# Channel attention and gated convolution on one core: depthwise weights converted early, later softmaxes partly on GpSimd, a new schedule of the score groups

## Chip, cores, metric

One Trainium2 chip, one core. The metric is the device time of a whole execution in microseconds (us); the kernel before took a median of 656.28 us over 3 runs (656.17 to 656.32). The engines are named as the profile names them: PE is TensorE (PEld its weight loads), DVE is VectorE, ACT is ScalarE, POOL is GpSimd, SP is the engine that issues the loads.

## What is computed

B = 4 batches, N = 6336 rows, C = 256 channels, float32; the three weights of the second half come as float64.

```python
qn = q / (norm(q, axis=1) + 1e-6)              # over the N rows, for each channel
kn = k / (norm(k, axis=1) + 1e-6)
s = kn.transpose(0, 2, 1) @ qn / tau           # 256 x 256 for each batch
a = exp(s - max(s)); a /= a.sum(-1) + 1e-9
x = v @ a
gate = sigmoid(causal depthwise conv of x, 5 taps: conv_w)
out = (gate * (x @ w_val)) @ w_out
```

## The kernel before

**Two passes that overlap.** For each batch a first pass reads q and k, adds up the scores k^T q in PSUM (s_ps) and the sums of squares for the norms. A softmax then makes the weights a, and the product of a with w_val, both kept as a high and a low half (float32r). The second pass reads v in 13 chunks of 508 rows, which are the steps: 4 batches x 13 = 52 steps. While the steps of a batch run, the scores of the next batch are added up between them.

**Score groups.** Rows of q and k come in 17 groups of a batch, of three 128-row pieces each (group 0 has two; group 3 two and the 64 left over). `score_group` splits pieces into a high half (a ScalarE cast, L223) and a low half (a GpSimd subtraction, L224), three float32r products each; "plain" pieces are multiplied as float32, without a split (`nw` pieces of a group). In batch 0 two pieces of a group are plain (all of the first four groups); in batch 1 two of each group below `LEAD`. The squares (L236, L240) are on ScalarE, their sums on VectorE and GpSimd (L246). `split_group` emits split and squares of the next group and issues loads (4 groups ahead), `run_group` emits the products of a group that has been split.

**Softmax.** `softmax(b)` is a generator; each `tick` emits its next piece at high priority. It joins the sums (L276), sums over partitions on TensorE (L281, L283) into a PSUM tile with a bank of its own, takes square roots there (L288), adds and inverts (L292 to L294), scales the scores (L299), takes the minimum (L301) and the exponentials (L304, with their sum z), scales them to a (L311), splits a (L314, L315), transposes it (L321) and multiplies it with w_val (L330 to L335).

**A step.** `step` n: sigmoid of chunk n, convolution of chunk n+1 (`conv`: product x_ps, first tap on ScalarE L395, four taps on VectorE L397), value product (`value`, L415), split of the gated value (`split_g`: g_hi on ScalarE L428, g_lo on GpSimd L429), transposes of v two chunks ahead (`transpose_v`, L371 to L373), and the output product of chunk n-1 (`finish`, L445, L455). PSUM has four banks for all tiles with tag "bank" (o_ps, t_ps, val_ps, the softmax's tiles) and two for x_ps.

**Weights.** The float64 weights are loaded as pairs of int32 words and decoded on VectorE (`decode`, L145 to L159, then L165, L167): w_val into wa, w_out into wb, the five taps (10 rows: 5 taps x 2 halves of the channels) into wk. The taps are then transposed on TensorE (L185) and copied to cw (L186). Taps and w_val are loaded at group 5 and decoded from group 9 of batch 0 on, one step of each for every group.

**What sets the order.** The code is written in the order of the main loop, and a scheduler then orders each engine's instructions; `tc.high_priority`, `tc.issue_after` and `behind(...)` (not before the marked instruction) steer it. How many groups run in a step comes from `due`, a straight line from the 22 groups done when the steps begin to all 68 at step 35: one or two a step, without a pause at the end of a batch. In each engine the instructions then start in that order.

## Time and profile before

| | us |
|---|---|
| median of 3 runs | 656.28 |
| the profiled execution | 654.72 |
| its span, first to last instruction | 652.9 |

The views used below: the page (busy time of each engine and its share of the span; the granted clock of TensorE in 40 slices, 9 being full speed to within a tenth), the waits (who waited for whom: us in total, times, longest), busy time by stretch of the span, groups of instructions by line (busy us, mean ns | idle us before them), the timeline (start, length, engine, line, instruction, and in brackets the idle time before it and what ended it), and the chain of waits that ended last (start, length, engine, line). In the timeline and in chains a row with x8 stands for eight instructions in a row. A float32 product of 256 columns is two records of the trace, one of float32r is one.

### The profile page before, as it was taken

How to read it: one execution, taken by the hardware profiler on the slowest of the kernel's cores; microseconds unless marked ns; L12 is line 12 of the kernel's file. 1: busy time of each engine (PE TensorE's matmuls, PEld its weight loads, DVE VectorE, ACT ScalarE, POOL GpSimd, SP SyncE). 2: the span in 40 equal slices, each digit the busy share in tenths (PEclk: the TensorE clock that was granted, in tenths of full speed). 3: DMA queues.
4: the chain of work that ended last, by engine and by line, in shares of the span. 5: the costliest groups of instructions: out<-in, count | busy, mean ns of one | idle time of the engine just before them, and what ended most of it. 6: DMA issues, size and time to landing. Idle time of an engine off the chain costs nothing.

```text
span 652.9 us, 10789 instructions
## 1 busy us (share of the span) xinstructions
PE 636.3 (97%) x4051; PEld 573.7 (88%) x4051; DVE 530.0 (81%) x849; ACT 472.5 (72%) x622; POOL 366.6 (56%) x177
## 2 busy tenths in 40 slices
PE   9899899999999999999998999999999999999996
PEld 7788799998988999999997998999999798888886
DVE  3998998887888688778887788778778889888884
ACT  5588978867898778678699777777777755655564
POOL 1674597956747759559575387766763122312221
PEclk9999999999999999999998999999999999999999
DMA  8989754454646464545563374553222343443213
GB/s 294 396 277 357 262 204 140 156 188 136 193 114 192 147 208 162 193 125 184 152 188 119 112 240 147 184 180 103 65 81 71 118 126 97 121 129 106 65 43 108
DMA packets 73817, 105.78 MB, mean 162 GB/s; under 512 B 4442, under 2 KB 55844, under 8 KB 73764
## 3 DMA queue, kind: packets, MB, share of 16 engines
q1 hardware_dynamic: 47988, 79.76, 37.0%
q10 hardware_dynamic: 25776, 25.32, 13.9%
q8 instruction: 32, 0.52, 0.3%
q14 instruction: 21, 0.17, 0.1%
HBM read 79.11 MB, written 25.95 MB: 161 GB/s over the span
## 4 chain that ended last, share of the span: by engine, by line
PE 79%; DVE 10%; ACT 5%; DMA 3%; issue 1%; POOL 1%; SPq 0%; ACTq 0%; DVEq 0%
PE o_ps L445 20%; PE x_ps L381 19%; PE val_ps L381 19%; PE s_ps L262 14%; PE t_ps L371 6%; DVE acc_ps L246 4%; DMA raw<-in_k_dram 2%; DVE gate L397 1%; ACT sq L240 1%; PE o_ps L330 1%; DMA out_dram<-o_sb 1%; ACT hi L223 1%; POOL hi L224 1%; DVE gate L415 1%; ACT gate L403 0%
## 5 line engine op out<-in xcount | busy, mean ns | idle before, releaser
L397 DVE SCALAR_TENSOR_TENSOR gate<-x_ps,cw,gate 128x508 f32<-128x508 f32 (+1 forms) x416 | 275.4, 718 | 14.2 <-ACT gate L395 13.1
L224 POOL TENSOR_TENSOR hi<-raw,hi 128x1536 fp32r<-128x1536 f32 (+2 forms) x65 | 182.9, 2816 | 115.4 <-ACT hi L223 115.4
L429 POOL TENSOR_TENSOR g_lo<-gate,g_hi 128x1016 fp32r<-128x1016 f32 (+1 forms) x50 | 116.7, 2335 | 143.1 <-ACT g_hi L428 133.2
L246 DVE TENSOR_TENSOR acc_ps<-acc_ps,sq 128x512 f32<-128x512 f32 (+1 forms) x142 | 98.7, 695 | 66.8 <-ACT sq L240 64.3
L381 PE MATMUL x_ps<-v_hi,w 128*128 128x512 f32 (+1 forms) x416 | 139.3, 394 | 0.3 <-DVE gate L397 0.3
L262 PE MATMUL s_ps<-hi 128*128 128x256 f32 (+1 forms) x918 | 133.4, 289 | 5.8 <-ACT hi L223 3.0
L381 PE MATMUL val_ps<-v_hi,w 128*128 128x508 f32 (+1 forms) x416 | 133.6, 383 | 0.7 <-ACT o_sb L455 0.7
L262 PEld LDWEIGHTS s_ps<-hi 128*128 128x128 f32 (+1 forms) x918 | 120.6, 190 | 11.8 <-POOL hi L224 3.8
L455 ACT COPY o_sb<-o_ps 128x512 f32<-128x512 f32 x99 | 58.2, 589 | 77.9 <-PE o_ps L445 77.7
L445 PE MATMUL o_ps<-wo_hi,g_hi 128*128 128x256 f32 x400 | 113.1, 283 | 0.2 <-DVE gate L415 0.2
L445 PE MATMUL o_ps<-wo_lo,g_hi 128*128 128x256 f32 x400 | 112.1, 280 | 0.0
L445 PE MATMUL o_ps<-wo_hi,g_lo 128*128 128x256 f32 x400 | 111.6, 279 | 0.0
L240 ACT ACTIVATE sq<-raw 128x1536 f32<-128x1536 f32 (+2 forms) x72 | 96.4, 1343 | 11.1 <-DVE acc_ps L246 8.6
L381 PEld LDWEIGHTS x_ps<-v_hi,w 128*128 128x128 f32 x416 | 78.2, 190 | 14.6 <-PE s_ps L262 0.4
L381 PEld LDWEIGHTS val_ps<-v_hi,w 128*128 128x128 f32 x416 | 77.2, 188 | 14.4 <-ACT o_sb L455 0.9
L395 ACT ACTIVATE gate<-x_ps,cw 128x508 f32<-128x508 f32 (+1 forms) x104 | 68.2, 670 | 19.8 <-PE x_ps L381 19.3
L372 ACT CAST v_hi<-t_ps 128x512 fp32r<-128x512 f32 (+1 forms) x104 | 55.6, 568 | 35.9 <-PE t_ps L371 35.9
L381 PE MATMUL x_ps<-v_lo,w 128*128 128x512 f32 (+1 forms) x208 | 80.3, 386 | 0.0
L381 PE MATMUL val_ps<-v_lo,w 128*128 128x508 f32 (+1 forms) x208 | 79.2, 381 | 0.0
L223 ACT CAST hi<-raw 128x1536 fp32r<-128x1536 f32 (+2 forms) x65 | 77.6, 1200 | 1.8 <-DMA raw<-in_k_dram 1.1
L415 DVE TENSOR_TENSOR gate<-val_ps,gate 128x508 f32<-128x508 f32 (+1 forms) x104 | 64.3, 658 | 18.0 <-ACT gate L403 12.8
L445 PEld LDWEIGHTS o_ps<-wo_hi,g_hi 128*128 128x128 f32 x400 | 75.2, 188 | 1.4 <-DVE gate L415 0.4
(99 smaller groups left out, 787.1 us busy)
## 6 DMA issues: line engine op xcount, KB each, us to landing
raw<-in_q_dram SPq DMA_DIRECT2D x60, 384.0 KB
raw<-in_k_dram SPq DMA_DIRECT2D x60, 384.0 KB
v_raw<-in_v_dram SPq DMA_DIRECT2D x44, 512.0 KB
out_dram<-o_sb ACTq DMA_DIRECT2D x47, 384.0 KB
out_dram<-o_sb ACTq DMA_DIRECT2D x47, 124.0 KB
raw<-in_q_dram SPq DMA_DIRECT2D x8, 256.0 KB
raw<-in_k_dram SPq DMA_DIRECT2D x8, 256.0 KB
v_raw<-in_v_dram SPq DMA_DIRECT2D x4, 384.0 KB
```

Of the source, the lines that this page charges most:

```text
L223: cast = nc.scalar.copy(hi[r, js, :, 0, :], rows_of[r, js])
L224: nc.gpsimd.tensor_tensor(hi[r, js, :, 1, :], rows_of[r, js], hi[r, js, :, 0, :].bitcast(F32), ALU.subtract)
L240: marks["SQ"] = nc.scalar.activation(sq[0:np_, ja:jb], rows_of[0:np_, ja:jb], AF.Square)
L246: eng.tensor_tensor(st[key][0:np_], st[key][0:np_], sq[0:np_, j], ALU.add)
L262: marks["SCORES"] = nc.tensor.matmul(st["s"][:, h, :], lhs, rhs, start=False, stop=stop and h == NH - 1 and n_ == len(ops) - 1)
L381: marks["PRODUCT"] = nc.tensor.matmul(ps, wt[:, which, ws, ch, hs], vs[:, ch, lo:hi_], start=ws == 0 and ch == 0 and vs is th, stop=ws == ...
L395: marks["TAP"] = nc.scalar.activation(gate[:, h, 0:w], x_ps[:, 0:w], AF.Copy, scale=cw[:, h:h + 1])
L397: marks["GATE"] = nc.vector.scalar_tensor_tensor(gate[:, h, 0:w], x_ps[:, tap:tap + w], cw[:, tap * NH + h:tap * NH + h + 1], gate[:, h, 0 ...
L415: nc.vector.tensor_tensor(gate[:, h, 0:w], vals[h][:, 0:w], gate[:, h, 0:w], ALU.mult)
L429: nc.gpsimd.tensor_tensor(gl[:, :, 0:w], gate[:, :, 0:w], gh[:, :, 0:w].bitcast(F32), ALU.subtract)
L445: nc.tensor.matmul(o_ps[:, u * C:(u + 1) * C], gs[:, h, off:off + P], ws[:, h, :], start=n_ == 0, stop=n_ == 3 * NH - 1)
L455: marks["ACT"] = nc.scalar.copy(o_sb[:, j:j + len(pair), :], o_ps[:, 0:len(pair) * C].rearrange("p (j c) -> p j c", c=C))
```

## The change

1. **Taps.** They and tau are loaded behind the first three groups, decoded right after group 0 is emitted, and transposed behind the first transposes of v in the first softmax, where their copy to cw now stands too.
2. **Way into the steps.** `LEAD` goes from 5 to 4: group 4 of batch 1 is split in whole and comes in the steps. Three steps instead of four of w_out's decoding stand before the first softmax's later part. The squares and adds of groups 4, 5 and 6 of batch 1 are owed: emitted behind the cast of the group after. In the first two steps a split waits for v's cast and the sigmoid too, and the sigmoid of step 0 stands ahead of the groups.
3. **Later softmaxes** (b > 0). The norms go from PSUM to SBUF with the square root, 1e-6 is added by ScalarE, the scores are scaled on GpSimd by two operations for each half instead of one on VectorE, a is scaled on GpSimd instead of ScalarE, its low half is taken on GpSimd instead of VectorE. In all softmaxes z lies in SBUF and 1e-9 is added on ScalarE.
4. **Schedule.** `due_after` has every batch's scores end four steps before its weights are due, runs no group in the step behind, then one in each of the next three steps.

```diff
-LEAD = 5
+LEAD = 4
+EARLY = 2
+OWE = 3
...
     def score_group(b, g):
...
+        if owed:
+            with tc.issue_after(cast.ins):
+                owed.pop()()
+        if b == 1 and LEAD <= g < LEAD + OWE:
+            def squares_and_adds():
...
+            owed.append(squares_and_adds)
...
     def softmax(b):
...
-        r, rk, z = n_ps[:, 0:C], n_ps[:, C:C + NH], n_ps[:, C + NH:C + 2 * NH]
-        marks["ACT"] = nc.scalar.activation(n_ps[:, 0:C + NH], n_ps[:, 0:C + NH], AF.Sqrt)
+        norms = n_ps if b == 0 else soft_p.tile([P, C + NH], F32, name="norms")
+        eng = nc.vector if b == 0 else nc.gpsimd
+        r, rk = norms[:, 0:C], norms[:, C:C + NH]
+        z = soft_p.tile([P, NH], F32, name="z")
+        note("ACT", nc.scalar.activation(norms[:, 0:C + NH], n_ps[:, 0:C + NH], AF.Sqrt))
...
-        nc.vector.tensor_scalar(n_ps[:, 0:C + NH], n_ps[:, 0:C + NH], 1e-6, None, ALU.add)
+        if b == 0:
+            nc.vector.tensor_scalar(norms[:, 0:C + NH], norms[:, 0:C + NH], 1e-6, None, ALU.add)
+        else:
+            nc.scalar.activation(norms, norms, AF.Identity, bias=small)
...
-        nc.vector.tensor_scalar(nk, rk, rtau, -1.0, ALU.mult, ALU.mult)
+        eng.tensor_scalar(nk, rk, rtau, -1.0, ALU.mult, ALU.mult)
         for h in range(NH):
-            nc.vector.scalar_tensor_tensor(s[:, h, :], s[:, h, :], nk[:, h:h + 1], r, ALU.mult, ALU.mult)
+            if b == 0:
+                nc.vector.scalar_tensor_tensor(s[:, h, :], s[:, h, :], nk[:, h:h + 1], r, ALU.mult, ALU.mult)
+            else:
+                nc.gpsimd.tensor_tensor(s[:, h, :], s[:, h, :], r, ALU.mult)
+                nc.gpsimd.tensor_scalar(s[:, h, :], s[:, h, :], nk[:, h:h + 1], None, ALU.mult)
...
-        nc.vector.tensor_scalar(z, z, 1e-9, None, ALU.add)
+        nc.scalar.activation(z, z, AF.Identity, bias=tiny)
...
-            nc.scalar.activation(a[:, h, :], s[:, h, :], AF.Copy, scale=rz[:, h:h + 1])
+            if b == 0:
+                nc.scalar.activation(a[:, h, :], s[:, h, :], AF.Copy, scale=rz[:, h:h + 1])
+            else:
+                nc.gpsimd.tensor_scalar(a[:, h, :], s[:, h, :], rz[:, h:h + 1], None, ALU.mult)
...
-        nc.vector.tensor_tensor(w[:, 0, 1], a, w[:, 0, 0].bitcast(F32), ALU.subtract)
+        eng.tensor_tensor(w[:, 0, 1], a, w[:, 0, 0].bitcast(F32), ALU.subtract)
...
+    load_taps()
+    prep.append(prepare_weights(2))
     for n in range(NG):
...
+        if n == 0:
+            for _ in prep.pop(0):
+                pass
...
-    for _ in range(4):
+    for _ in range(3):
         next(out_words, 0)
     tick()
     with behind("PE", "ACT", "DVE"):
         run_group()
         for h in range(NH):
             transpose_v(*step(0), h)
+        turn_taps()
     with behind("ACT"):
         split_group()
-        split_group()
-    with behind("SQ"):
-        tick()
+    tick()
     tick()
...
     tick()
     tick()
+    with behind("ACT"):
+        split_group()
     tick()
...
-    last = len(all_steps) - NC - 4
+    LAG = 4
+    ends = [NC * b - LAG for b in range(1, B)]
+    def due_after(n):
+        done, start = NG + LEAD, 0
+        for b, stop in enumerate(ends):
+            goal = NG * (b + 2)
+            if n + 1 >= stop:
+                done, start = goal, stop
+                continue
+            if b and n + 1 <= start + LAG:
+                return done + max(n - start, 0) if n >= start else done
+            if b:
+                done, start = done + LAG - 1, start + LAG
+            return done + -(-(goal - done) * (n + 1 - start) // (stop - start))
+        return total
...
-        due = NG + LEAD + -(-(total - NG - LEAD) * (n + 1) // (last + 1))
-        turns = min(due, total) - (issued - len(ready))
+        turns = due_after(n) - (issued - len(ready))
+        if n == 0:
+            sigmoid(*now)
         for turn in range(turns):
             if turn == 0:
                 run_group()
-                with behind("ACT"):
+                with behind(*(["ACT", "VH", "SIG"] if n < EARLY else ["ACT"])):
                     split_group()
         tick()
-        with end(n + 1):
-            sigmoid(*now)
+        if n:
+            with end(n + 1):
+                sigmoid(*now)
```

The two constants `tiny` (1e-9) and `small` (1e-6) are written by VectorE at the start. Line numbers of the kernel after differ: 246 becomes 265, 397 becomes 434, 429 becomes 466, 224 becomes 234, 145 to 167 become 152 to 174.

What this does to the order of VectorE's instructions in batch 0: the kernel before, in the middle of batch 0 (acc_ps are the sums of squares; wk and wk_raw the taps).

```order
L246 TENSOR_TENSOR acc_ps<-acc_ps,sq 128x512 x3
L145 TENSOR_SCALAR wk<-wk_raw 10x128
L246 TENSOR_TENSOR acc_ps<-acc_ps,sq 128x512
L147 SCALAR_TENSOR_TENSOR wk_raw<-wk_raw,wk 10x128
L246 TENSOR_TENSOR acc_ps<-acc_ps,sq 128x512
L149 TENSOR_SCALAR wk<-wk_raw 10x128
L151 TENSOR_SCALAR wk<-wk 10x128
L153 TENSOR_SCALAR wk<-wk 10x128
L155 SCALAR_TENSOR_TENSOR wk<-wk_raw,wk 10x128
L246 TENSOR_TENSOR acc_ps<-acc_ps,sq 128x512
```

And the kernel after, from the first two sums of batch 0 on:

```order
L265 TENSOR_TENSOR acc_ps<-acc_ps,sq 128x512 x2
L152 TENSOR_SCALAR wk<-wk_raw 10x128
L265 TENSOR_TENSOR acc_ps<-acc_ps,sq 128x512
L154 SCALAR_TENSOR_TENSOR wk_raw<-wk_raw,wk 10x128
L156 TENSOR_SCALAR wk<-wk_raw 10x128
L158 TENSOR_SCALAR wk<-wk 10x128
L265 TENSOR_TENSOR acc_ps<-acc_ps,sq 128x512
L160 TENSOR_SCALAR wk<-wk 10x128
L265 TENSOR_TENSOR acc_ps<-acc_ps,sq 128x512
L162 SCALAR_TENSOR_TENSOR wk<-wk_raw,wk 10x128
```

The taps' decoding moved from between the sums of groups in the middle of batch 0 to between those of groups 1 to 3.

VectorE once more, from the first softmax into the first step: the kernel before, from group 3's 64 rows left over to the last tap of step 0 (w_raw and wb are w_out, gate from x_ps is a tap; row L335 is the low half of the fused weights, v_lo that of v):

```order
L246 TENSOR_TENSOR acc_ps<-acc_ps,sq 64x512
L335 TENSOR_TENSOR w<-o_ps,w 128x512
L373 TENSOR_TENSOR v_lo<-t_ps,v_hi 128x512
L246 TENSOR_TENSOR acc_ps<-acc_ps,sq 128x512
L373 TENSOR_TENSOR v_lo<-t_ps,v_hi 128x512
L397 SCALAR_TENSOR_TENSOR gate<-x_ps,cw,gate 128x508
L246 TENSOR_TENSOR acc_ps<-acc_ps,sq 128x512
L397 SCALAR_TENSOR_TENSOR gate<-x_ps,cw,gate 128x508 x3
L246 TENSOR_TENSOR acc_ps<-acc_ps,sq 128x512
L397 SCALAR_TENSOR_TENSOR gate<-x_ps,cw,gate 128x508 x2
L246 TENSOR_TENSOR acc_ps<-acc_ps,sq 128x512
L397 SCALAR_TENSOR_TENSOR gate<-x_ps,cw,gate 128x508 x2
```

The kernel after, up to the last tap of step 0:

```order
L265 TENSOR_TENSOR acc_ps<-acc_ps,sq 128x512
L166 TENSOR_TENSOR w_raw<-w_raw,wb 128x512
L265 TENSOR_TENSOR acc_ps<-acc_ps,sq 128x512
L434 SCALAR_TENSOR_TENSOR gate<-x_ps,cw,gate 128x508
L265 TENSOR_TENSOR acc_ps<-acc_ps,sq 64x512
L434 SCALAR_TENSOR_TENSOR gate<-x_ps,cw,gate 128x508 x3
L372 TENSOR_TENSOR w<-o_ps,w 128x512
L434 SCALAR_TENSOR_TENSOR gate<-x_ps,cw,gate 128x508 x2
L410 TENSOR_TENSOR v_lo<-t_ps,v_hi 128x512
L434 SCALAR_TENSOR_TENSOR gate<-x_ps,cw,gate 128x508
L410 TENSOR_TENSOR v_lo<-t_ps,v_hi 128x512
L434 SCALAR_TENSOR_TENSOR gate<-x_ps,cw,gate 128x508
```

Fewer sums of squares stand between the taps, and the fused weights' low half (L372 now) has moved behind step 0's first four taps.

GpSimd around the softmax of batch 2, before (hi is the low half of a score group in GpSimd's rows, g_lo that of the gated value):

```order
L352 MEMSET v_raw 4x256
L224 TENSOR_TENSOR hi<-raw,hi 128x4x256
L429 TENSOR_TENSOR g_lo<-gate,g_hi 128x1016
L224 TENSOR_TENSOR hi<-raw,hi 128x6x256
L429 TENSOR_TENSOR g_lo<-gate,g_hi 128x1016
L224 TENSOR_TENSOR hi<-raw,hi 128x6x256
```

After, in the same place (nk is the scale by 1/norm and tau, s the scores, a the softmax's result):

```order
L466 TENSOR_TENSOR g_lo<-gate,g_hi 128x1016
L234 TENSOR_TENSOR hi<-raw,hi 128x4x256
L326 TENSOR_SCALAR nk<-norms,rtau 128x2
L389 MEMSET v_raw 4x256
L332 TENSOR_TENSOR s<-s,norms 128x256 x2
L333 TENSOR_SCALAR s<-s,nk 128x256 x2
L466 TENSOR_TENSOR g_lo<-gate,g_hi 128x1016
L348 TENSOR_SCALAR a<-s,rz 128x256 x2
L352 TENSOR_TENSOR w<-a,w 128x512
L466 TENSOR_TENSOR g_lo<-gate,g_hi 128x1016
```

The scalings now stand between three g_lo, and of the score groups only the next batch's group 0 (hi of 4x256) stands here, ahead of them.

More of the change, by code (lines that the diff above doesn't have):

```diff
@@ L106 @@
     tc.keep_in_program_order(nc.scalar.activation(dummy, ones[:, 0:1], AF.Sqrt))
+    tiny = const.tile([P, 1], F32, name="tiny")
+    nc.vector.memset(tiny, 1e-9)
+    small = const.tile([P, 1], F32, name="small")
+    nc.vector.memset(small, 1e-6)
     rtau = const.tile([P, 1], F32, name="rtau")
@@ L131, in load_weights, with load_taps @@
                           in_=src.rearrange("(h p) e -> p h e", p=P))
-        if part == 0:
-            raw = const.tile([K * NH, P, WORDS], I32, name="wk_raw") if WORDS == 2 else wk.rearrange("p (n o) -> p n o", o=1)
-            w_raw["taps"] = raw
-            src = conv_w.bitcast(I32) if WORDS == 2 else conv_w
-            nc.sync.dma_start(out=raw.rearrange("p n o -> p (n o)"), in_=src.rearrange("k (h n) -> (k h) n", h=NH))
-            nc.sync.dma_start(out=tau_sb, in_=tau.broadcast_to([P, 1]))
+    def load_taps():
+        raw = const.tile([K * NH, P, WORDS], I32, name="wk_raw") if WORDS == 2 else wk.rearrange("p (n o) -> p n o", o=1)
+        w_raw["taps"] = raw
+        src = conv_w.bitcast(I32) if WORDS == 2 else conv_w
+        nc.sync.dma_start(out=raw.rearrange("p n o -> p (n o)"), in_=src.rearrange("k (h n) -> (k h) n", h=NH))
+        nc.sync.dma_start(out=tau_sb, in_=tau.broadcast_to([P, 1]))
     def decode(raw, f):
@@ L170, in prepare_weights @@
     def prepare_weights(part):
-        if part:
+        if part == 1:
             if WORDS == 2:
                 yield from decode(w_raw[1], wb)
-                nc.scalar.copy(wo_hi.rearrange("p h e -> p (h e)"), w_raw[1][:, :, 1].bitcast(F32))
+                marks["WO"] = nc.scalar.copy(wo_hi.rearrange("p h e -> p (h e)"), w_raw[1][:, :, 1].bitcast(F32))
                 nc.vector.scalar_tensor_tensor(wo_lo.rearrange("p h e -> p (h e)"), w_raw[1][:, :, 0], 2.0 ** -35, wb,
@@ L181, in prepare_weights, with turn_taps @@
             return
-        yield from whole_words(w_raw[0], wa)
+        if part == 0:
+            yield from whole_words(w_raw[0], wa)
+            return
         yield from whole_words(w_raw["taps"], wk)
+        tc.keep_in_program_order(nc.vector.reciprocal(rtau, tau_sb))
+    def turn_taps():
         taps = ps.tile([P, 512], F32, name="taps", tag="bank")
@@ L186, in prepare_weights @@
         nc.scalar.copy(cw, taps[:, 0:K * NH])
-        yield
-        tc.keep_in_program_order(nc.vector.reciprocal(rtau, tau_sb))
-    state = {}
+    state, owed = {}, []
     def score_group(b, g):
@@ L226, in score_group @@
         where = {}
+        if owed:
[3 more added lines that the diff above has]
+            def squares_and_adds():
+                for np_, j0, nj in parts:
+                    nc.scalar.activation(sq[0:np_, j0:j0 + nj], rows_of[0:np_, j0:j0 + nj], AF.Square)
+                adds()
+            owed.append(squares_and_adds)
         with tc.issue_after(cast.ins) if cast else nullcontext():
-            squares = [(np_, j0, j0 + nj) for np_, j0, nj in parts]
-            for key in ("acc", "side"):
+            squares = [(np_, j0, j0 + nj) for np_, j0, nj in parts] if not owed else []
+            for key in ("acc", "side") if not owed else ():
                 if key not in st["begun"]:
@@ L248, in score_group @@
         late = b == 1 and 0 < g < LEAD
-        if not late:
+        if not late and not owed:
             adds()
@@ L272, in softmax, with note @@
     def softmax(b):
+        def note(key, ins):
+            if b == 0:
+                marks[key] = ins
         st = state.pop(b)
@@ L303, in softmax @@
         for h in range(NH):
[L304 removed]
+            note("ACT", nc.scalar.activation(s[:, h, :], s[:, h, :], AF.Exp, scale=-1.0, bias=m[:, h:h + 1], accum_out=z[:, h:h + 1]))
         yield
[L306 removed]
+        nc.scalar.activation(z, z, AF.Identity, bias=tiny)
         rz = soft_p.tile([P, NH], F32, name="rz")
@@ L324, in softmax @@
         at = soft_p.tile([P, NH, C], F32, name="at")
-        marks["ACT"] = nc.scalar.copy(at.rearrange("p h c -> p (h c)"), at_ps)
+        note("ACT", nc.scalar.copy(at.rearrange("p h c -> p (h c)"), at_ps))
         yield
@@ L333, in softmax @@
         awf = aw_ps.rearrange("p (h c) -> p h c", h=NH)
-        marks["ACT"] = nc.scalar.copy(w[:, 1, 0], awf)
+        note("ACT", nc.scalar.copy(w[:, 1, 0], awf))
         marks["DVE"] = nc.vector.tensor_tensor(w[:, 1, 1], awf, w[:, 1, 0].bitcast(F32), ALU.subtract)
@@ L402, in sigmoid @@
         gate = gates[b, i]
-        nc.scalar.activation(gate[:, :, 0:w], gate[:, :, 0:w], AF.Sigmoid)
+        marks["SIG"] = nc.scalar.activation(gate[:, :, 0:w], gate[:, :, 0:w], AF.Sigmoid)
     def value(b, i):
```

6 lines of the change are left out of this document (3 added, 3 removed).

## Prediction

> **What bounds it now.** I read the page's busy times first, then the waits of TensorE, then busy times by stretch, and last the timeline and the chain of waits inside the stretches that lose time.
>
> ```profile
> PE 636.3 (97%) x4051; PEld 573.7 (88%) x4051; DVE 530.0 (81%) x849; ACT 472.5 (72%) x622; POOL 366.6 (56%) x177
> PEclk9999999999999999999998999999999999999999
> ```
>
> TensorE is busy for 636.3 of 652.9 us, so the kernel can gain only where TensorE waits (16.6 us) or runs on a lowered clock. Part of those 16.6 us are the first loads and the last stores, which the change leaves alone. The longest waits and the stretches that hold the rest:
>
> ```profile
> PE s_ps L262 <- ACT hi L223: 3.0, 2, 2.7
> PE taps L185 <- DVE wk L167: 2.6, 1, 2.6
> ```
>
> ```profile
> core 0: us, PE busy (x) PEld busy (x) DVE busy (x) ACT busy (x) POOL busy (x), PEclk, DMA share, GB/s
> 18.80:52.70 33.90, 30.88 (x165) 27.43 (x165) 32.83 (x52) 22.49 (x24) 23.61 (x18) 0.95 0.95 336
> 52.70:82.00 29.30, 27.08 (x158) 23.50 (x157) 26.31 (x45) 26.23 (x39) 14.71 (x9) 1.00 0.90 304
> 174.00:204.00 30.00, 29.19 (x175) 25.27 (x174) 24.15 (x41) 27.27 (x39) 13.63 (x7) 1.00 0.44 126
> 336.00:368.00 32.00, 29.31 (x183) 26.33 (x183) 27.05 (x46) 25.37 (x36) 14.60 (x6) 0.95 0.45 141
> 488.00:520.00 32.00, 30.75 (x190) 26.87 (x189) 27.56 (x47) 24.23 (x38) 10.77 (x6) 1.00 0.29 87
> 600.00:640.00 40.00, 40.00 (x249) 35.75 (x248) 33.72 (x53) 23.43 (x36) 9.63 (x4) 1.00 0.26 72
> ```
>
> The columns are the stretch, its length, the busy time of each engine with its instruction count, the granted clock and the DMA load. These are the scores of batch 0, the way into the first step, the three later softmaxes, and undisturbed steps to compare with. TensorE loses 3.0, 2.2, 0.8, 2.7 and 1.25 us in the first five (length minus PE busy), about 10 us. In two of them the mean clock is 0.95.
>
> **Taps early (batch 0).** In batch 0 TensorE works through one group after another; the weight loads of each group's plain rows mark the pace.
>
> ```profile
> 23.50 1.60 PEld L262 LDWEIGHTS s_ps<-raw 128*128 128x128 f32 x8
> 25.95 1.60 PEld L262 LDWEIGHTS s_ps<-raw 128*128 128x128 f32 x8
> 31.89 2.62 PEld L262 LDWEIGHTS s_ps<-raw 128*128 128x128 f32 x8
> 50.75 1.60 PEld L262 LDWEIGHTS s_ps<-raw 128*128 128x128 f32 x8
> ```
>
> Undisturbed, a group takes 25.95 - 23.50 = 2.45 us. From 25.95 to 50.75 there are eight groups: 19.6 us at that pace, 24.8 measured, so 5.2 us are lost. The taps' transpose stands in the middle (the 2.6 us wait above); the group behind it takes 2.62 us where the others take 1.60, and the clock says why:
>
> ```profile
> 27.40:34.60 7.20, 4.61 (x19) 3.82 (x17) 7.20 (x13) 2.82 (x6) 3.06 (x3) 0.76 0.98 379
> ```
>
> The granted clock over that stretch is 0.76. The Trainium skill, "TensorE: Matmul & The Clock Gate", section "What's actually happening", has the clock fall only after about 3.4 us of idleness; by that rule a wait of 2.6 us would cost nothing more and removing it would bring the waits alone, 3.0 us in this stage, instead of 5.2. The row decides against the rule.
>
> Now the taps are transposed behind the transposes of v, so TensorE no longer meets them here. Does VectorE let it go faster? Its chain has no gap between these two rows (start, length):
>
> ```profile
> 18.76 0.70 DVE acc_ps L246
> 52.74 0.68 DVE acc_all L276
> ```
>
> ```profile
> 18.00:31.00 13.00, 0.27 (x1) 0.18 (x1) 6.07 (x9) 0.98 1.03 397
> ```
>
> That is 34.0 us, and the row below them, of the tile wk alone, puts 6.07 us of it on decoding the taps. Without them VectorE needs 28 us and is done around 46.7; TensorE starts its last group at 50.75 - 5.2 = 45.6 and ends it around 48: TensorE binds, narrowly. The decode goes to where VectorE waited for the first squares:
>
> ```profile
> 5.38 0.70 DVE L246 TENSOR_TENSOR acc_ps<-acc_ps,sq 128x512 f32<-128x512 f32 x1 [3.84 <-ACT sq L240]
> 9.63 1.43 DVE L246 TENSOR_TENSOR acc_ps<-acc_ps,sq 128x512 f32<-128x512 f32 x2 [3.54 <-ACT sq L240]
> ```
>
> These waits hide it, so I cost it at nothing; if the taps' small load landed late, the adds queued behind the first decode step would slip, and with them ScalarE's next squares, by at most the 5.2 us won. The two loads, moved ahead of group 3's rows on SP, delay those by two issues like this one:
>
> ```profile
> 12.53 0.36 SPq L136 DMA_DIRECT2D wk_raw<-in_moe_conv_w_dram  x1
> ```
>
> So 0.7 us at most, partly hidden by what is queued ahead (groups 0 to 2). I take -4.7 us, bounds -2.5 and -5.2.
>
> **Into the first step (LEAD 4, owed squares, order of splits).** Today VectorE is the chain from the first softmax to step 0's last tap, and TensorE waits for GpSimd's low half of a whole group, then for the tap.
>
> ```profile
> 79.06 2.41 PE L262 MATMUL s_ps<-hi 128*128 128x256 f32 x18 [1.95 <-POOL hi L224]
> 81.72 0.47 PE L381 MATMUL x_ps<-v_hi,w 128*128 128x512 f32 x1 [0.25 <-DVE gate L397]
> ```
>
> In VectorE's order, 12 adds stand between the joined sums of batch 0 and step 0's last tap before, 8 now, and one more decode step: 4 x 0.69 - 0.42 = 2.3 us less, so step 0 ends about 4.7 + 2.3 = 7 us earlier. But TensorE's order now has less to do meanwhile: groups 4 and 5 of batch 1 come later, and four instructions stand right behind results of VectorE or ScalarE (the low half of the weights, L315; the fused weights' low half, L335; the cast of group 4; step 1's v low half). I estimate half a us each, from waits of 0.25 to 1.95 above: 2 us new for 2.2 old. The deferred squares of groups 4 to 6, the splits held behind v's casts and the sigmoid, and that sigmoid moved ahead of the groups only change who is late, since ScalarE is busy 26.2 of 29.3 us here; one decode step of w_out more behind the joined sums is in the sum. Bounds: -2.2 (no wait is left) and +3 (each of the four costs over 1 us). A certain gain is small: group 4's two plain rows become split rows.
>
> ```profile
> L262 PE MATMUL s_ps<-raw 128*128 128x256 f32 (+1 forms) x188 | 46.2, 394 | 0.0
> 170.63 2.04 PE s_ps L262 x17
> ```
>
> A plain row is four records of 46.2 / 188 = 0.246, or 0.98 us; a split row six of 2.04 / 17 = 0.12, or 0.72. Two rows: -0.5 us. ScalarE and GpSimd get two rows more to split, which their idle time in this stretch hides. Stage: -0.5.
>
> **Later softmaxes.** The costly one is the second (336 to 368):
>
> ```profile
> 349.60 1.28 ACT L304
> 353.06 1.38 ACT hi L223
> 354.87 4.34 PE x_ps L381 x12
> 381.95 2.77 PE x_ps L381 x12
> ```
>
> In ScalarE's queue a group's cast stands behind table load, exponentials and two copies, and TensorE's next product waits 2.7 us for it (the wait at the top); then twelve x_ps products take 4.34 instead of 2.77 us. Together 4.3 us. With the new schedule the step behind a batch's last group runs no group and the next three run one each, so no cast is due here. (The diff's words "a step sooner" hold only for batch 3, step 34 instead of 35; batch 1 ends in step 8 as before, batch 2 half a step sooner in step 21. The empty step is what counts.) The stretch at 488 shows such a softmax without casts: it still loses 1.25 us, on VectorE, since the chain there goes through gates and scalings. Now part of VectorE's share goes:
>
> ```profile
> L299 DVE SCALAR_TENSOR_TENSOR s<-s,nk,o_ps 128x256 f32<-128x256 f32 x8 | 3.5, 476 | 0.0
> L315 DVE TENSOR_TENSOR w<-a,w 128x512 fp32r<-128x512 f32 x4 | 2.7, 683 | 0.0
> L294 DVE RECIPROCAL o_ps<-o_ps 128x256 f32<-128x256 f32 x4 | 7.1, 1764 | 0.1
> L288 ACT ACTIVATE o_ps<-o_ps 128x258 f32<-128x258 f32 x4 | 1.5, 370 | 0.0
> L311 ACT ACTIVATE a<-s,rz 128x256 f32<-128x256 f32 x8 | 3.6, 500 | 2.3 <-DVE rz L308 2.3
> L246 POOL TENSOR_TENSOR acc<-acc,sq 128x512 f32<-128x512 f32 x50 | 65.6, 1312 | 13.1 <-ACT sq L240 11.9 <-DMA raw<-in_q_dram 0.6
> ```
>
> VectorE loses 2 x 0.48 + 0.68 = 1.6 us per softmax and three smaller instructions; it keeps the long reciprocal. ScalarE loses 2 x 0.50 and gains an add of 258 columns (the square root of as many took 0.37) and one of 2 columns (no more than that, I take 0.2): -0.4. GpSimd gains six operations of 256 columns and one of 512. The nearest row is 1.31 us for 512 columns, so 0.66 for 256 if it scales, 1.31 at most: 6 x 0.66 + 1.31 + 0.2 = 5.5 us, up to 9.4. GpSimd is 56% busy and has no group to split in the empty step. The bank of norms is also given back after the square root instead of after the last reciprocal. I take 0.5 us left per softmax (between none and the 1.25 above): -(0.8 + 4.3 + 1.25) + 1.5 = -4.85; bounds -6.35 and, by the last rival but one, beyond zero.
>
> The two constants are written while VectorE waits at the start: nothing. In the last steps no order changes.
>
> **Sum.** -4.7 - 0.5 - 4.85 = -10.0 us. The profiled execution took 654.7 us (its span 652.9), so 644.7; the median of the runs is 656.28, 1.56 above it, so **646.3 us**.
>
> **Rivals.** *Everything hidden*: TensorE never waits in these stages; -5.2 - 2.2 - 0.5 - 6.35 = -14.2, 642.0 us. For it speaks that mid-kernel stretches show PE busy throughout; against, the tight ScalarE queue.
> *VectorE keeps the prologue*: the earlier end of batch 0 runs into the same gates and TensorE waits there instead; only -0.5 and the softmaxes stay: 650.9 us. For it: VectorE's unbroken chain, to which the last wait before 81.72 leads.
> *Softmax waits come back*: as large as the old ones, by a cast or gate in another place; 656.28 - 5.2 = 651.1 us.
> *GpSimd's chain is late (slower)*: the scalings now stand in GpSimd's queue between two g_lo, each waiting for ScalarE:
>
> ```profile
> L429 POOL TENSOR_TENSOR g_lo<-gate,g_hi 128x1016 fp32r<-128x1016 f32 (+1 forms) x50 | 116.7, 2335 | 143.1 <-ACT g_hi L428 133.2
> 340.48 2.74 PE val_ps L381 x12
> 366.56 2.84 PE o_ps L445 x24
> 373.49 0.87 PE t_ps L371 x8
> ```
>
> TensorE has between the norms and the transposes of a some 14.7 us of work in the last softmax (val, t_ps, x_ps, o_ps, val, x_ps: 2.7 + 0.9 + 2.8 + 2.8 + 2.7 + 2.8), and scores beside it in the others. The chain, end to end, is square root and table 1.65, add 0.37, reciprocals 1.95, GpSimd's scalings 0.2 + 4 x 0.66, minimum 0.7, table and exponentials 2.4, sum and reciprocal 0.4, a 2 x 0.66: 11.6, and 2 us of queueing (estimate): 13.6. At 1.31 us per operation (+3.9) and two g_lo of 2.34 in between (+4.7) it is 22.2, and TensorE waits about 6 us each time (7.5 in the last, less in the others). Then -5.2 - 6.35 + 18 = +6.5, 662.8 us. It decides from a wait of 3.9 us each time, a chain of about 20 us.
>
> Beside it: the Trainium skill, "GPSIMD Engine Reference", section "Engine selection", sends elementwise work to VectorE because GpSimd takes about twice as long with two inputs; the trace agrees (1.31 against 0.69 us for 512 columns).
>
> *It doesn't do what it says*: TensorE's waits are elsewhere by then and nothing moves, 656.3.
>
> **Chances.** Forecast (643.5 to 649.5) 0.50, everything hidden 0.10, VectorE keeps the prologue 0.15, softmax waits come back 0.13, GpSimd late 0.08, nothing moves 0.04. A measurement of this kernel tells about 0.2% (1.3 us) from no change. Faster 0.88, same 0.04, slower 0.08. The range 642.5 to 652.0 takes in the forecast and the two middle rivals and leaves out the others.
>
> **What would show it.** Right: no wait of TensorE for wk and a clock of 1.00 from 20 to 50 us; TensorE's last group of batch 0 at about 46 instead of 50.75; no ScalarE wait and no lowered clock around the second softmax; GpSimd's scalings near 0.66 us. Wrong: VectorE still without a gap and TensorE waiting for w or v_lo between 55 and 80 us by more than 2 us; TensorE waiting at the transposes of a; operations of 256 columns on GpSimd over 1.3 us.

## The result, and the profile after

The changed kernel takes 651.20 us (median of 4 runs, 650.71 to 652.02), the kernel before beside it 656.22 (4 runs, 654.63 to 656.32): a ratio of 0.993, 95% interval 0.9911 to 0.995. That is faster by 5.0 us. The forecast was 646.3, a gain of 10.0; the measured time lies in the range (642.5 to 652.0), and the sign is right, but half of the gain didn't come. The profiled execution took 650.71 us with a span of 648.9.

The page of the changed kernel: busy time of each engine, and the granted clock in 40 slices.

```profile
PE 633.7 (98%) x4055; PEld 571.0 (88%) x4055; DVE 524.5 (81%) x832; ACT 472.1 (73%) x623; POOL 386.8 (60%) x201
PEclk9999999999999999999999999999999999999999
```

TensorE is busy for 2.6 us less (636.3 before), which is mostly the lowered clock that is gone (about 1.6 us around the second softmax and 1.0 in batch 0), and waits for 15.2 us instead of 16.6. Where it gained and where not is in the same stretches as before:

```profile
core 0: us, PE busy (x) PEld busy (x) DVE busy (x) ACT busy (x) POOL busy (x), PEclk, DMA share, GB/s
18.80:52.70 33.90, 31.20 (x175) 27.35 (x174) 31.47 (x45) 24.39 (x27) 23.58 (x18) 1.00 0.96 357
52.70:82.00 29.30, 28.08 (x155) 23.58 (x154) 25.16 (x43) 23.95 (x37) 10.90 (x6) 1.00 0.72 250
174.00:204.00 30.00, 29.70 (x180) 26.17 (x179) 24.54 (x39) 25.67 (x40) 18.83 (x13) 1.00 0.46 141
336.00:368.00 32.00, 31.00 (x201) 27.96 (x200) 25.35 (x41) 25.28 (x39) 17.46 (x9) 1.00 0.35 111
488.00:520.00 32.00, 31.11 (x189) 27.13 (x188) 26.00 (x41) 23.32 (x37) 13.89 (x12) 1.00 0.31 96
```

The three softmaxes (last three rows) lose 0.3, 1.0 and 0.9 us instead of 0.8, 2.7 and 1.25, and the clock of the second is 1.00 instead of 0.95: as forecast. Batch 0 (first row) still loses 2.7 us instead of 3.0, though the wait for the taps is gone. Its end is best read where TensorE starts the norms' product, the first thing behind the last group. Before and after (start, length):

```profile
53.48 0.70 PE L281 MATMUL o_ps<-acc_all,ones 128*128 128x256 f32 x2
```

```profile
52.40 0.60 PE L305 MATMUL o_ps<-acc_all,ones 128*128 128x256 f32 x2
```

That is 1.1 us earlier instead of the 4.7 forecast. The timeline of TensorE shows new waits in batch 0, and that of VectorE and ScalarE what is behind them:

```profile
37.15 0.86 PE L281 MATMUL s_ps<-hi 128*128 128x256 f32 x5 [1.07 <-POOL hi L234]
40.40 0.38 PE L281 MATMUL s_ps<-hi 128*128 128x256 f32 x1 [0.65 <-ACT hi L233]
41.75 0.86 PE L281 MATMUL s_ps<-hi 128*128 128x256 f32 x5 [0.97 <-POOL hi L234]
```

```profile
38.35 1.48 ACT L259 ACTIVATE sq<-raw 128x1536 f32<-128x1536 f32 x1 [3.76 <-DVE acc_ps L265]
```

```profile
37.57 13.65 DVE L265 TENSOR_TENSOR acc_ps<-acc_ps,sq 128x512 f32<-128x512 f32 x18
51.33 0.69 DVE L300 TENSOR_TENSOR acc_all<-acc_ps,acc 128x512 f32<-128x512 f32 x1
```

Read from the last rows up: VectorE is full up to 51.3. When the decode of the value weights is over (37.6), 18 adds are still to be done. Squares have two buffers, so ScalarE waits 3.76 us for an add before it can square the next group; the casts behind that square come late, GpSimd's low halves with them, and TensorE waits at 40.40 and 41.75. (Its wait at 37.15 lies ahead of that: ScalarE had waited for adds twice before, 1.77 and 0.62 us, and the GpSimd subtraction that TensorE needs took 1.71 us itself.) The releaser that a wait of TensorE names, POOL or ACT, is two steps from the cause.

Why VectorE is full, in spite of 6 us less to do, is in single steps of the decode. VectorE's rows, and GpSimd's in the same time:

```profile
29.80 1.16 DVE L162 SCALAR_TENSOR_TENSOR wa<-w_raw,wa 128x512 int32<-128x512 int32 x1
31.48 0.42 DVE L164 TENSOR_SCALAR w_raw<-w_raw 128x512 int32<-128x512 int32 x1
31.81 0.69 DVE L265 TENSOR_TENSOR acc_ps<-acc_ps,sq 128x512 f32<-128x512 f32 x1
32.41 1.46 DVE L166 TENSOR_TENSOR w_raw<-w_raw,wa 128x512 int32<-128x512 int32 x1
34.39 1.58 DVE L172 SCALAR_TENSOR_TENSOR wa<-w_raw,wa 128x512 f32<-128x512 int32 x1
```

```profile
28.95 1.46 POOL L234 TENSOR_TENSOR hi<-raw,hi 128x512 fp32r<-128x512 f32 x1
32.05 1.27 POOL L234 TENSOR_TENSOR hi<-raw,hi 128x512 fp32r<-128x512 f32 x1 [1.64 <-ACT hi L233]
34.16 1.27 POOL L265 TENSOR_TENSOR acc<-acc,sq 128x512 f32<-128x512 f32 x1 [0.84 <-ACT sq L259]
```

L166 ends at 33.87, 0.55 us behind the end of GpSimd's operation (33.32); L172 at 35.97, 0.54 behind (35.43); L162 at 30.96, 0.55 behind (30.41). They look as if they had done nothing until GpSimd was through. Seven of the ten steps are so, where four were in the kernel before. L164, which meets no GpSimd operation, takes 0.42. The adds, whose accumulator lies in PSUM, take 0.69 whatever GpSimd does.

### The profile page after: what moved, and what is told of

The parts are those of the page before. It is cut to its first block, busy times and chain, and to the rows that moved or that the text cites. A ratio compares the mean times of both kernels' runs of the same rounds, so it can differ in the third digit from the quotient of the medians.

```text
span 648.9 us, 10823 instructions
## 1 busy us (share of the span) xinstructions
PE 633.7 (98%) x4055; PEld 571.0 (88%) x4055; DVE 524.5 (81%) x832; ACT 472.1 (73%) x623; POOL 386.8 (60%) x201
## 4 chain that ended last, share of the span: by engine, by line
PE 80%; ACT 6%; DMA 5%; DVE 4%; issue 2%; POOL 1%; SPq 1%; ACTq 0%; POOLq 0%
PE o_ps L482 20%; PE x_ps L418 19%; PE val_ps L418 19%; PE s_ps L281 15%; PE t_ps L408 6%; DMA raw<-in_k_dram 2%; DMA w_raw<-in_moe_w_val_dram 1%; DVE gate L434 1%; PE o_ps L367 1%; POOL hi L234 1%; ACT sq L259 1%; DMA v_raw<-in_v_dram 1%; SPq L83 1%; DVE acc_ps L265 1%; DMA out_dram<-o_sb 1%
## 5 line engine op out<-in xcount | busy, mean ns | idle before, releaser
L434 DVE SCALAR_TENSOR_TENSOR gate<-x_ps,cw,gate 128x508 f32<-128x508 f32 (+1 forms) x416 | 277.0, 719 | 10.8 <-ACT gate L432 8.8
L234 POOL TENSOR_TENSOR hi<-raw,hi 128x1536 fp32r<-128x1536 f32 (+2 forms) x65 | 184.8, 2847 | 96.5 <-ACT hi L233 92.2
L281 PE MATMUL s_ps<-hi 128*128 128x256 f32 (+1 forms) x930 | 135.2, 289 | 3.8 <-POOL hi L234 3.0
L259 ACT ACTIVATE sq<-raw 128x1536 f32<-128x1536 f32 (+3 forms) x69 | 91.8, 1336 | 7.5 <-DVE acc_ps L265 6.2
```

Of the source, the lines that this page charges most:

```text
L234: nc.gpsimd.tensor_tensor(hi[r, js, :, 1, :], rows_of[r, js], hi[r, js, :, 0, :].bitcast(F32), ALU.subtract)
L259: marks["SQ"] = nc.scalar.activation(sq[0:np_, ja:jb], rows_of[0:np_, ja:jb], AF.Square)
L281: marks["SCORES"] = nc.tensor.matmul(st["s"][:, h, :], lhs, rhs, start=False, stop=stop and h == NH - 1 and n_ == len(ops) - 1)
L434: marks["GATE"] = nc.vector.scalar_tensor_tensor(gate[:, h, 0:w], x_ps[:, tap:tap + w], cw[:, tap * NH + h:tap * NH + h + 1], gate[:, h, 0 ...
```

## The experiments

Ratios are to the kernel before, run beside; in brackets the 95% interval. "Start" is the start of the norms' product in the profiled execution: 53.48 before, 52.40 after.

**The parts alone.** e1 is before with the taps' part, e2 before with the later softmaxes and the schedule, e4 both, with the first step left as it was.

```diff
+    load_taps()
+    prep.append(prepare_weights(2))
...
+        if n == 0:
+            for _ in prep.pop(0):
+                pass
...
             transpose_v(*step(0), h)
+        turn_taps()
```

> The kernel before with one part of the change: the taps are loaded first, decoded after group 0 and turned behind v; everything else as before. Theory V (VectorE still sets the end of batch 0, because the decode of the value weights and the adds fill it and the freed 6 us are mostly taken again): the norms' product starts about 1 us earlier than before (52.4 instead of 53.5), median 654.9 to 655.7 against 656.2. Rival F (the part is worth the 4.7 us of the forecast, and the edits to the first step lose them again): norms' product near 49, median 651 to 652.

> The kernel before with the later softmaxes' part alone: scalings on GpSimd, norms in SBUF, the scores of a batch a step sooner; taps and first step as before. Theory V: the waits around the second to fourth softmax nearly go, 4 us, median 651.8 to 652.6. Rival F says the same here; a rival by which the whole gain of the change comes from the start would give 655 to 656.

> The kernel before with the taps' part and the later softmaxes' part, but the first step as before (lead of five groups, split order and owed squares of before). Theory V: the two add up, 5 us, median 651 to 651.5, so that the edits into the first step are worth nothing to within 0.5. Rival F: 647 to 648, the edits into the first step having cost 3 to 4 us.

| | median us | ratio | start |
|---|---|---|---|
| e1 taps | 653.75 | 0.9974 [0.9962, 0.9986] | 51.80 |
| e2 softmaxes, schedule | 651.40 | 0.9943 [0.993, 0.9955] | 53.88 |
| e4 both | 650.87 | 0.9925 [0.9912, 0.9938] | 54.02 |

The taps bring about 1.7 us (interval 0.9 to 2.5) of the 4.7 forecast, somewhat more than theory V said; the softmaxes bring 3.7 (3.0 to 4.6) of 4.85; both together as much as the whole change. (e2 leaves batch 0 as it was and starts at 53.88 instead of 53.48, so a start tells to about half a us.) So the edits to the first step, forecast at -0.5, are worth nothing that can be measured, and rival F falls. e4's profiled execution has the late start for a reason of its own, to which the last section comes back.

**Is it VectorE's work?** e3 is the changed kernel without the decode of the value weights; a constant stands in their place, so the output is not the reference's.

```diff
+    nc.vector.memset(wa, 0.01)
...
-            yield from whole_words(w_raw[0], wa)
```

> The changed kernel without the ten VectorE steps that decode the value weights (they are loaded, but a constant stands in their place, so the products with them are of a constant). It frees about 10.5 us of VectorE between 23.6 and 37.7. Theory V: TensorE's waits of 35 to 43 go, its batch 0 runs at 2.45 us a group, the norms' product starts at 49 to 50 instead of 52.4, median 648 to 649. Rival D (the loads of q and k, pushed back by the two small loads, set batch 0): norms' product stays at 52 or so, median 651.

```profile
18.80:52.70 33.90, 33.90 (x198) 30.85 (x198) 27.27 (x42) 28.36 (x33) 23.77 (x19) 1.00 1.02 374
```

```profile
48.39 0.60 PE L305 MATMUL o_ps<-acc_all,ones 128*128 128x256 f32 x2
```

TensorE has no gap in the stretch of batch 0, the start is 4.0 us earlier than in the changed kernel, the median 646.81 (0.9865 [0.9851, 0.9879]): 4.4 us below it. The loads of q and k are nearly as late as there (the fourth group's first one is issued at 4.81 us, at 5.41 in the changed kernel and at 3.57 before), so rival D falls: they don't hold TensorE up here.

**Its amount, or the queue of squares?** e5 has a third buffer for the squares.

```diff
-        sq = split_p.tile([P, GROUP, 2, C], F32, name="sq", bufs=2)
+        sq = split_p.tile([P, GROUP, 2, C], F32, name="sq", bufs=3)
```

> The changed kernel with three buffers for the squares instead of two, so that ScalarE can square a group, and so cast the next, before VectorE has added the group two before. Theory V (VectorE's amount of work sets the end of batch 0: it has no gap until its last add at 51.2): TensorE's waits of 35 to 43 shrink or move, but the last add stays where it is and the norms' product starts within 0.5 us of 52.4; median within 1 us of 651.2. Rival Q (the queue of two buffers, not the amount of work, is what holds TensorE up): the norms' product starts at 49.5, median 648 to 649.

```profile
52.05 0.70 PE L305 MATMUL o_ps<-acc_all,ones 128*128 128x256 f32 x2 [1.34 <-DVE acc_all L300]
```

651.34 (0.9935 [0.9922, 0.9947]): no gain. Now that ScalarE can run ahead, TensorE ends its groups earlier and then waits, 1.34 us, for VectorE's sum itself. The name in the bracket is at last the right one: the amount of VectorE's work sets the end.

**The small loads.** e6 puts the loads of taps and tau on ScalarE's queue, so that those of q and k are issued as before.

```diff
-        nc.sync.dma_start(out=raw.rearrange("p n o -> p (n o)"), in_=src.rearrange("k (h n) -> (k h) n", h=NH))
-        nc.sync.dma_start(out=tau_sb, in_=tau.broadcast_to([P, 1]))
+        nc.scalar.dma_start(out=raw.rearrange("p n o -> p (n o)"), in_=src.rearrange("k (h n) -> (k h) n", h=NH))
+        nc.scalar.dma_start(out=tau_sb, in_=tau.broadcast_to([P, 1]))
```

> The changed kernel with the taps and tau loaded by ScalarE's queue, so that the loads of q and k go out on SyncE's queue as they did before (the fourth group at 3.57 instead of 5.41). Theory V: TensorE's start is mended (8.5 of 10 us busy instead of 7.58, 0.4 us earlier at the second group), the end of batch 0 moves by at most 0.5, median 650.5 to 651.2. Rival D (the late loads of q and k keep batch 0 from gaining): norms' product at 50 or so, median 648 to 649.

```profile
9.18 3.04 PE L281 MATMUL s_ps<-raw 128*128 128x256 f32 x13 [1.74 <-DMA raw<-in_k_dram]
```

The start of TensorE was not mended, it got worse: the second group starts at 9.18 instead of 8.49 (8.12 before). Yet the median is 649.82 (0.9911 [0.9898, 0.9925]), start 51.45. The taps were decoded by 7.2 us, before GpSimd has its first add or subtraction, in the waits for the first squares; VectorE's tenth add ends at 18.8 us instead of 19.6, and its joined sum starts 0.6 us earlier (50.71). The value weights' decode takes 9.9 us as there. The intervals of e6 and of the changed kernel overlap; the earlier start is seen in one profile only.

**Fewer adds for VectorE.** e7 gives a third of each group's adds to GpSimd throughout batch 0.

```diff
-                nw, nv = GROUP - 1, 2 + g % 2
+                nw, nv = GROUP - 1, 2
```

> The changed kernel with two rows of each group added on VectorE and the third on GpSimd throughout batch 0; as it stands VectorE adds all three in every second group from the fifth on. VectorE sheds six or seven adds of 0.69 us (4.5 us), GpSimd takes them at 1.29 us each (8 us; it is idle for 10 of the 35 us). Theory V: the norms' product starts 2 to 3 us earlier, at 49.5 to 50.5, median 648 to 649.5. The rival by which GpSimd's subtractions come late instead: no gain, 651 to 653, with longer waits of TensorE for GpSimd's low parts.

```profile
51.09 1.65 DVE L154 SCALAR_TENSOR_TENSOR w_raw<-w_raw,wb 128x512 int32<-128x512 int32 x1
53.12 0.68 DVE L300 TENSOR_TENSOR acc_all<-acc_ps,acc 128x512 f32<-128x512 f32 x1
```

```profile
49.45 2.73 POOL L265 TENSOR_TENSOR acc<-acc,sq 128x512 f32<-128x512 f32 x2
```

653.22 (0.9965 [0.9952, 0.9977]), worse than the changed kernel. The joined sum needs GpSimd's adds as well as VectorE's, and GpSimd's last ones end at 52.18 (50.71 in the changed kernel): now GpSimd is late, with VectorE's adds done by 50.0. Besides, the first steps of the output weights' decode slip ahead of the sum and meet those adds (1.65 us for what takes 0.70 in the changed kernel), so the sum starts 0.9 us later still. TensorE waits 2.22 us for it, and its longest wait for a low half is 1.9 us instead of 1.1, as the rival had it. GpSimd is not spare capacity here.

**The decode elsewhere.** e10 moves seven of the ten steps on the value weights behind the first softmax, and the output weights' decode behind that softmax's last step.

```diff
+            pool, tag = ((const, "wa_raw"), (w_p, "o_sb"))[part]
...
-            prep.append(prepare_weights(0))
...
-    out_words = prepare_weights(1)
+    out_words = prepare_weights(0)
...
+    with behind("DVE"):
+        for _ in prepare_weights(1):
+            pass
```

> The changed kernel with the decode of the value weights mostly moved out of batch 0 to where the output weights are decoded now (behind the first softmax), and that of the output weights behind the first softmax's last step; the value weights get a buffer of their own. Seven of the ten steps leave the stretch from 18 to 51 us. Theory V: norms' product at 49 to 49.5, 3 us earlier; of these up to 2 are lost again if the product of the turned attention with the value weights (at 68.7 now) waits for the decode; median 648 to 650. Rival D: norms' product at 52, median 651 to 653.

The start is 48.14, even 1 us earlier than expected, and the median 659.25 (1.0052 [1.0039, 1.0064]), slower than before. The decode of the output weights now stands beside whole-group subtractions of GpSimd. VectorE's rows, then GpSimd's:

```profile
77.16 3.10 DVE L158 TENSOR_SCALAR wb<-wb 128x512 int32<-128x512 int32 x1
81.75 3.87 DVE L162 SCALAR_TENSOR_TENSOR wb<-w_raw,wb 128x512 int32<-128x512 int32 x1
```

```profile
76.46 3.52 POOL L234 TENSOR_TENSOR hi<-raw,hi 128x1536 fp32r<-128x1536 f32 x1 [0.69 <-PE x_ps L418]
81.39 3.68 POOL L234 TENSOR_TENSOR hi<-raw,hi 128x1536 fp32r<-128x1536 f32 x1
```

Steps of 0.42 and 0.69 us take 3.10 and 3.87, and end 0.28 and 0.55 us behind GpSimd's operation (79.98 and 85.07). v's low half is queued behind them on VectorE, and TensorE waits 8.6 us for it. A miss as a version, it is the clearest view of the mechanism. (That batch 0 ends earlier agrees with e3; rival D falls again.)

**The same steps with a PSUM operand.** If a step waits because all its operands are in SBUF, it must stop waiting when the word that is worked on lies in PSUM. e11 does that; no step is dropped, and the hold behind "SUM" (the joined sum) keeps the output weights' steps where they stand in the changed kernel.

```diff
-            yield from decode(raw, w)
-            nc.vector.scalar_tensor_tensor(w, raw[:, :, 0], 2.0 ** -35, w, ALU.mult, ALU.mult)
+            np_, width = w.shape
+            f = ps.tile([P, 512], F32, name="x_ps", bufs=2)[0:np_, 0:width]
+            yield from decode(raw, f)
+            nc.vector.scalar_tensor_tensor(f, raw[:, :, 0], 2.0 ** -35, f, ALU.mult, ALU.mult)
...
-            nc.vector.tensor_tensor(w, w, raw[:, :, 1].bitcast(F32), ALU.add)
+            nc.vector.tensor_tensor(w, f, raw[:, :, 1].bitcast(F32), ALU.add)
...
-    for _ in range(3):
-        next(out_words, 0)
+    with behind("SUM"):
+        for _ in range(3):
+            next(out_words, 0)
```

> The changed kernel with the word that the decode of the value weights and taps works on in a PSUM bank (of the two that the gate's product uses later) instead of in SBUF; nine of the ten steps so have an operand or the result in PSUM. Same steps, same place; the first steps of the output weights' decode are held behind the sum of the accumulators, where they stand now. The ten steps on the value weights took 9.9 us in the changed kernel, single ones between 0.42 and 1.58. Theory P (a VectorE step whose operands are all in SBUF waits while GpSimd works on SBUF; one with PSUM does not, as the adds into PSUM, always 0.69, show): each step takes 0.7 or less beside GpSimd, 6.6 us in all, VectorE is done some 3 us earlier, the norms' product starts at 50 to 50.7 instead of 52.4, median 649 to 649.8. Rival (the steps on integers are of uneven length for a reason of their own): they stay near 1.2 us, no gain, 651 or more, since the one-input steps lose their 0.42. The Trainium skill, "SBUF — State Buffer", section "Who interferes with whom", says that VectorE instructions with two SBUF inputs, or in a mode that uses two ports, contend with GpSimd and that the one that comes second blocks fully; that is theory P.

Steps that took 1.16, 1.46 and 1.58 us, now in PSUM, and a GpSimd operation beside the last two (L166 above is L166 here, L172 is L175):

```profile
29.03 0.69 DVE L162 SCALAR_TENSOR_TENSOR x_ps<-w_raw,x_ps 128x512 int32<-128x512 int32 x1
31.16 0.68 DVE L166 TENSOR_TENSOR w_raw<-w_raw,x_ps 128x512 int32<-128x512 int32 x1
31.76 0.69 DVE L175 SCALAR_TENSOR_TENSOR x_ps<-w_raw,x_ps 128x512 f32<-128x512 int32 x1
```

```profile
30.46 1.34 POOL L237 TENSOR_TENSOR hi<-raw,hi 128x512 fp32r<-128x512 f32 x1 [0.76 <-ACT hi L236]
31.98 1.28 POOL L268 TENSOR_TENSOR acc<-acc,sq 128x512 f32<-128x512 f32 x1 [0.18 <-ACT sq L262]
```

```profile
48.47 0.63 PE L308 MATMUL o_ps<-acc_all,ones 128*128 128x256 f32 x2
```

All ten take 0.42 to 0.69, 6.6 us in all instead of 9.9, though eight of them start while a GpSimd operation runs. The start is 48.47, within 0.1 of the kernel that doesn't decode at all, and the median 648.28 (0.9884 [0.987, 0.9897]): faster than before by 1.2% and, the intervals being apart, faster than the changed kernel. Theory P holds, the rival falls. The gain is larger than theory P expected (start 50 to 50.7, 649 to 649.8): VectorE starts its joined sum at 47.66, 3.7 us earlier instead of some 3, of which the taps' steps, no longer lengthened either, are a part.

**On top of it.** e12 adds e6's queue, e13 the third buffer of squares to that; e14 is e11 with the third buffer and with the small loads, on SyncE's queue, behind those of the fourth and fifth group.

```diff
+        if n == 0:
+            load_taps()
             for _ in prep.pop(0):
```

> The kernel with the decode in PSUM and, besides, the taps and tau loaded by ScalarE's queue. If the two gains are of different kinds (VectorE's time, and q and k landing earlier) they add up: 1.4 us below the kernel with the decode in PSUM alone, 647.5 to 648.5, norms' product near 49.5. If one bound hides the other: within 0.5 of it.

> As the kernel with the decode in PSUM and the taps on their own queue, with a third buffer for the squares. With VectorE's work cut, the two buffers may be what holds ScalarE and so TensorE up: then TensorE runs from 10 us on without a wait, the norms' product starts at 48.4 to 49, as it did without any decode of the value weights, and the median is 646.5 to 647.5. If VectorE's amount of work still binds: no difference to the kernel with two buffers, to within 0.5.

> The kernel with the decode in PSUM (648.28), on SyncE's queue again, with a third buffer for the squares, and with the two small loads of taps and tau issued after those of the fourth and fifth group instead of ahead of them. If the small loads cost the start (TensorE busy 7.50 of the first 10 us, 8.94 in the kernel before, where they came later), TensorE is busy 8.5 us or more there, and the norms' product starts at 47.4 to 48 instead of 48.47; median 647.2 to 647.9. If the start does not hang on them, as the kernel with its own queue for them suggests (7.04 us): norms' product at 48.4 or later and the median within 0.5 of 648.3.

| | median us | ratio | TensorE's second group | start |
|---|---|---|---|---|
| e11 | 648.28 | 0.9884 [0.987, 0.9897] | 8.52 | 48.47 |
| e12 | 651.12 | 0.9928 [0.9914, 0.9941] | 10.22 | 52.56 |
| e13 | 648.41 | 0.9884 [0.9871, 0.9898] | 10.27 | 50.15 |
| e14 | 648.37 | 0.9894 [0.9878, 0.9911] | 8.20 | 48.72 |

None beats e11, and the hopes for e12 (647.5 to 648.5), e13 (646.5 to 647.5) and e14 (647.2 to 647.9) were missed; e14 came out as its second expectation has it, within 0.5 of 648.3. In e12 the scheduler put the next batch's first products ahead of the norms' product; TensorE waits there, and the norms' product starts 2.4 us later than in e13:

```profile
50.93 0.50 PE L289 MATMUL s_ps<-zeros 128*128 128x512 f32 x1 [0.68 <-ACT s L305]
52.56 0.59 PE L308 MATMUL o_ps<-acc_all,ones 128*128 128x256 f32 x2
```

e14 mends TensorE's start as expected (busy 8.96 of the first 10 us), and at the end of batch 0 TensorE waits for VectorE's sum:

```profile
48.72 0.70 PE L308 MATMUL o_ps<-acc_all,ones 128*128 128x256 f32 x2 [0.42 <-DVE acc_all L303]
```

So with the decode in PSUM the two engines end batch 0 within half a microsecond of each other in this profile, and the better start of TensorE brought nothing that can be measured.

## Why the prediction was wrong by half

**Taps early: -4.7, came -1.1 to -1.7** (the start in the changed kernel, the median in e1). The step that failed is "Without them VectorE needs 28 us and is done around 46.7", and with it "TensorE binds, narrowly". The subtraction took rows of one order of work for fixed durations. VectorE was done at 51.3 (it starts the joined sum at 51.33 instead of 52.74), because of two things that the runs put in its place. First, the decode of the value weights got longer, from 7.9 us (its ten rows before) to 9.9, since other steps of it fell beside GpSimd's operations: a VectorE step with all its operands in SBUF waits them out (e10), and doesn't with one in PSUM (e11). The 6.07 us of the taps' decode were such waits in good part; in e11 the same steps take 0.20 to 0.28 us each. Second, "These waits hide it, so I cost it at nothing": in VectorE's order the first step of the taps stands behind the second add, and so behind both long waits.

```profile
5.38 0.70 DVE L265 TENSOR_TENSOR acc_ps<-acc_ps,sq 128x512 f32<-128x512 f32 x1 [3.83 <-ACT sq L259]
10.04 0.70 DVE L265 TENSOR_TENSOR acc_ps<-acc_ps,sq 128x512 f32<-128x512 f32 x1 [3.97 <-ACT sq L259]
```

The taps' steps, between 10.8 and 18.2 us, found only shorter waits to fill (1.06, 0.21, 0.80 and 0.54 us before), and three of them took 0.72, 0.90 and 0.84 us beside GpSimd. Eight adds were done by 18.2 where ten had been, 1.4 us. VectorE gained 1.4 of 6.1 us; the 2.0 and the 1.4 us are 3.4 of the 4.7 that are missing. By the rows, about 1 us of the rest is the adds themselves: between decode steps one costs 0.60 us from its start to the next (31.81 to 32.41), in a row of adds 0.76 (13.76 for the last 18), and from 18.2 us on 24 of them stand in rows instead of 17; no run tests this.

The Trainium skill, "SBUF — State Buffer", section "Who interferes with whom", says that VectorE with two SBUF inputs, or in a mode that uses two ports, and GpSimd take an exclusive lock, and that the later one blocks fully for the whole instruction. The runs agree: of the steps of 512 columns, those with two inputs end 0.54 to 0.56 us behind the GpSimd operation that they meet, those with one 0.28 or 0.29. The prediction didn't weigh that rule, nor the rows of the kernel before that show it; "VectorE still without a gap" did stand among its signs of being wrong.

The two loads, "0.7 us at most, partly hidden": they took 1.8 us to issue (0.77 and 1.01) and TensorE's second group starts 0.4 us later. e14, which issues them later and is no faster than e11, gives no sign that this cost anything.

**The clock.** Right for this kernel: it is 1.00 from 20 to 50 us once the 2.6 us wait is gone. But the new waits of 1.07, 0.65 and 0.97 us did not lower it, and in e4 such waits did (last section), so what lowers it stays open.

**First step: -0.5, came about 0** (e4 against the changed kernel, whose intervals are nearly the same), inside the bounds. The prediction put half a us on each of four instructions. One of these waits is there: TensorE waits 1.02 us for the low half of the weights. It is the same mechanism:

```profile
64.04 1.78 DVE L352 TENSOR_TENSOR w<-a,w 128x512 fp32r<-128x512 f32 x1
```

```profile
63.92 1.34 POOL L234 TENSOR_TENSOR hi<-raw,hi 64x512 fp32r<-64x512 f32 x1 [2.39 <-DMA raw<-in_q_dram]
```

GpSimd is through at 65.26, the step ends at 65.82, 0.56 later; 0.68 us of work took 1.78. It is still so in e11, and no run took it away.

**Later softmaxes: -4.85, came -3.7** (e2, interval -3.0 to -4.6; in the changed kernel the three stretches lose 2.6 us less by waits and the 1.6 us of the lowered clock are gone). Mechanism right, the term a little too large: 0.3, 1.0 and 0.9 us are left instead of 0.5 each. These are waits of the output product for ScalarE's copy of the transposed a, which gives the bank back (0.3 and 1.0), and in the last softmax of an x_ps product for VectorE (0.9). Forecast and rival "GpSimd late" hung on the 256-column operations; they took:

```profile
L333 POOL TENSOR_SCALAR s<-s,nk 128x256 f32<-128x256 f32 x6 | 5.5, 925 | 0.0
L348 POOL TENSOR_SCALAR a<-s,rz 128x256 f32<-128x256 f32 x6 | 5.5, 924 | 9.5 <-DVE rz L342 9.5
L332 POOL TENSOR_TENSOR s<-s,norms 128x256 f32<-128x256 f32 x6 | 4.3, 744 | 1.4 <-DVE norms L324 1.4
```

0.74 and 0.93 us, between the 0.66 taken and the bound of 1.31, and TensorE doesn't wait at the transposes of a themselves.

**The rivals.** "Softmax waits come back" (651.1) and "VectorE keeps the prologue" (650.9) are nearest in time, but neither happened. The waits in the three softmaxes went from 4.75 to 2.2 us. And the prologue's mechanism, an earlier end of batch 0 lost again at the gates, needs an earlier end: batch 0 itself ended only 1.1 us earlier. That the measured time lies in the range is luck: the range reaches to 652.0 for the sake of these two.

## What to carry to other kernels

Before taking work off a full engine and subtracting its row, see whether the row's single instructions are as long as they are alone: those that end a fixed time behind another engine's instruction are waits, and come back with whatever is moved into their place. Work on VectorE that runs beside GpSimd should have one operand or the result in PSUM, if a bank is free; that was worth more here (2.9 us) than moving the taps, although a step with one input then takes 0.69 us instead of the 0.42 that it takes undisturbed. And where a wait names an engine that was only late itself, a third buffer or the removal of one link shows who is behind it.
